# Linear attention block with a squared-ReLU MLP on one core: column parts split on chip, one more tile turned by moves, three tiles normalised on ScalarE

## The chip, the cores and the metric

The kernel runs on one core of a Trainium2 chip. The metric is the time of one execution on the device in microseconds (us): 410.08 us is the median of three runs (409.76 to 411.25). The core has five engines with instruction streams of their own: TensorE (PE in the profile; its weight loads are PEld), VectorE (DVE), ScalarE (ACT), GpSimd (POOL) and SyncE (SP), which here issues nearly all transfers. Each engine works its stream in order; waits between engines are by semaphores.

## What is computed

x is 2048 x 512. It is normalised by rows, goes through a linear attention with 32 heads of 16 channels and, beside it, through an MLP with 1376 hidden units, and the sum of x and both is returned.

```python
xn = layernorm(x)                       # no gain, no bias
q, k, v = xn @ wqkv                     # split in three, 32 heads of 16
phi = lambda t: where(t > 0, t + 1, exp(t)) + 1e-6
kv = einsum("bhsd,bhse->bhde", phi(k), v);  z = phi(k).sum(tokens)
attention = (phi(q) @ kv) / (phi(q) @ z + 1e-6) @ wo
mlp = relu(xn @ w1 + b1)**2 @ w2 + b2
return x + attention + mlp
```

## The kernel before

Float32 products are made from two parts of each factor, a high part (rounded to the TensorE's fp32r form) and a low part (the rest): three matmuls high x high, high x low, low x high. So every operand is "split": a copy on ScalarE makes the high part (`copy("act", ...)`, L111), a subtraction on VectorE or GpSimd the low part (L119, L122).

The 2048 tokens are 16 tiles of 128, in four blocks of four tiles. There are two phases.

Phase 1 (the loop `for i in range(2, NT)`, L801, with tiles 0 and 1 ahead of it) makes, for each tile i:
- statistics (`measure`, L234 and L235, on VectorE), the reciprocal root (`roots`, L245 and L246, mostly on GpSimd), the normalised tile `xp[i]` (`normalise`). In `normalise` tiles below NPE = 8 are normalised on VectorE (L268), the others on ScalarE (L258), for which a short VectorE operation first makes the bias (L254).
- the turned tile (channels on the partitions), needed as "column parts" for the projections. Tiles below NDVE = 4 are turned by TensorE: four transposes (`turned_pe`, L308) into PSUM. The others are turned "by moves": `regroup` (L281) stores the tile to DRAM (`via`), four DMAs (`move`, L289) bring it back with its 32-row blocks in another order into `xg`, and a VectorE transposition of 32x32 blocks (`turn`, L293) finishes it. `transposed` then gives three closures: `high` (ScalarE, L324), `low` (VectorE, L327), and `keep_t`, which stores the turned tile in DRAM (`xTd`, L336) for blocks 0 and 1.
- the projection to k, twelve matmuls (`project`, L369), and phi of it (`phi`: Relu on ScalarE L360, Exp on ScalarE L362, sum on VectorE L364), split in `parts` (L377).
- the token parts (`tokens`: high on ScalarE L111, low on GpSimd L119). The last channel of each normalised tile is first set to one (`ones`, L346, GpSimd), so that the sum of phi(k) comes out of the same product.
- `kx(i)`, twelve matmuls (L389) that add tokens x phi(k) to four PSUM banks.

In round i of the loop TensorE does the projection of tile i and then kx(i - 1); a round is 24 matmuls. The tiles of x come in four loads of two tiles (x8, x10, x12, x14) behind a load of four (x4) and single ones. SyncE issues these loads, the stores and the moves from one queue in program order.

The column parts of a block of four tiles lie in `xsb[0]` or `xsb[1]` (names xs0 and xs1, h and l), which hold two blocks at a time. When a block is done that phase 2 handles second (blocks 0 and 1), its column parts are stored to DRAM (`xsd`, L811, in rounds 4 and 7; 1 MB for each of the four).

Phase 2 (the loop `for n in range(2)`, L941) handles the blocks in pairs, 3 and 2 first, then 1 and 0. For each pair the projection to q and w1 runs as a product of 2x2 blocks with seven instead of eight products (`product`, L488, with operands `aop`, `T`, sums `S`), then squares and splits the hidden chunks (`hidden_2`, L450, L119), multiplies by w2 (`mlp_2`, L130), adds the attention (`add_attention`, L130), the residual (L1054), and stores (L1058). At the end of n = 0 the loop at L1285 walks the hidden chunks of the second block, with steps of other work on ScalarE and VectorE put between by a list (AE). There the operands for n = 1 are prepared: the turned blocks come back from DRAM into `f1` and `f2` (L1254, L1255), from which sums and differences are made (`sums_of`, L671, L111, L122); the column parts are loaded into `x1` and `x2` from `xsd` (L1302); the last chunk of w1 is loaded (L184) and split (`zs`), the first chunk of q is loaded (L714) and split (`operands_first`). The last four steps (L1318) add the attention tile by tile and split the last two hidden chunks (`wait_for`), and the closing loop multiplies those by w2, tile by tile. n = 1 then begins with `plain_1` (pz, L130), which reads x1 and the last chunk of w1, and with the first product (L488).

Of the kernel before, what the change touches and what calls it, by code (L numbers as in the profile page):

```python
# [13 lines left out]
P = 128  # L14
# [4 lines left out]
def kernel(  # L19
# [41 lines left out]
    NPE = 2 * TB  # L61
    NDVE = NPE - 4
    WARM = 11
# [36 lines left out]
    def f32(ap):  # L100
        return ap.bitcast(F32)
# [44 lines left out]
    xTd = [dram.tile([P, NJ, BT], F32, name=f"xTd{b}") for b in range(NB // 2)]  # L146
    xsd = [[dram.tile([P, NJ, BT], F32, name=f"xsd{b}{u}") for u in "hl"] for b in range(NB // 2)]
    w2s, wos = {}, {}
# [99 lines left out]
    def normalise(tiles, st, mv, y):  # L248

        n = len(tiles)  # L250
        r, u = (y[:, k, :n] for k in range(2))
        if tiles[-1] >= NPE:

            nc.vector.scalar_tensor_tensor(u, mv[:, :n, 0], -1.0, r, op0=OP.mult, op1=OP.mult)  # L254
# [7 lines left out]
        for k, i in enumerate(tiles):  # L262
            o, src = xp[i], xr[i]
            if i >= NDVE:

                o, src = o.rearrange("p g (j c) -> p g j c", j=NJ), gjc(src)
            if i < NPE:
                nc.vector.tensor_scalar(o, src, mv[:, k, 0:1], r[:, k:k + 1], op0=OP.subtract, op1=OP.mult)  # L268
                if i in groups:
                    regroup(i)  # L270
            else:
                later.append(lambda a=(i, o, src, k): last(*a))
# [74 lines left out]

    def tokens(i, el="pool"):
        tok[i] = pair(f"tok{i}")
        h, l = tok[i][:, 0], tok[i][:, 1]  # L350
        src = xp[i]
        if i >= NDVE:
            h, l, src = gjc(h), gjc(l), src.rearrange("p g (j c) -> p g j c", j=NJ)
        split(h, l, src, "act", el)
        if NDVE <= i + 1 < NT:
            ones(i + 1)

    def phi(ps, p, mid=lambda: None, late=lambda: None):
# [187 lines left out]
    for i0 in range(0, NT, TB):  # L546
        a = first_xp[i0]
        for k in range(TB):
            xp[i0 + k] = a[:, k]
        if i0 + TB <= NDVE:  # L550
            continue
        n = TB if i0 >= NPE else TB // 2
        if i0 < NPE:
            single = work.tile([P, 2, 512], F32, name=f"xg{i0}s", tag="r0")
            for k in range(2):
                i = i0 + k
                xp[i], xg[i] = (t.rearrange("p (g n) -> p g n", g=NJ) for t in (xp[i], single[:, k]))
                groups[i] = [xp[i], xg[i]]
# [62 lines left out]
    heads_k(3)  # L621
    low1(1)
    for u in range(2):
        some(0, u, (2,))
# [10 lines left out]
    rests_k("dve", 3)  # L635
    fourth = statistics(3)
    roots(*fourth)
    high, low, keep2 = transposed(2)
# [3 lines left out]
    rest(3)  # L642
    load_x(8, x8[:, :2])
    load_x(10, x8[:, 2:])
    load_x(12, two("x12"))
    project(2, pks[2], wk, HL)
    single = group(4)
    soon = group(5)
    normalise(*fourth)
    phi_k(0, pks[0])  # L650
# [5 lines left out]
    normalise(*single)  # L656
    load_x(14, two("x14"))
    parts(1)
    tokens(1, "dve")
    measure(soon)  # L660
    roots(*soon)
    keep2()
# [121 lines left out]

    def small_chunk(z):
        t = raw_1(NF - 1)
        return lambda: split(z[:, 0], z[:, 1], t, "act", "dve")

# [12 lines left out]
    for i in range(2, NT):  # L801
# [4 lines left out]
        move()  # L806
        if i in (4, 7):

            b = i // 7
            for u in range(2):  # L810
                nc.sync.dma_start(xsd[b][u], f32(cols(b * TB)[u]))  # L811
        if i == 9:
# [6 lines left out]
        high = low = keep_t = lambda: None  # L819
        if i < NDVE:  # L820
            high, low, keep_t = transposed(i + 1)
        later = normalise(*soon) if i == 3 else []

        soon_turned = transposed(i + 2) if 11 <= i and i + 2 < NT else ()

        def mid():
            high()
            more(i)

        def late():  # L830
            low()
            more(i)
# [19 lines left out]
        if i != 3:  # L852
            later = normalise(*soon) if soon else []
        parts(i)
        keep_t()
        if i == 2:
            tokens(2)
        if i + 1 < NT:
            tokens(i + 1)
        run(*later)  # L860
        if NDVE < i + 2 < 13:
            run(*transposed(i + 2))
# [3 lines left out]
        if i + 2 in (4, 6, 8, 10):  # L866
            ahead[i + 2] = group(i + 6, i + 7)
        if i < 10:
            measure(ahead[(i + 2) // 2 * 2], i % 2)
        soon = ahead.get(i + 1, ())  # L870
# [70 lines left out]
    for n in range(2):  # L941
# [343 lines left out]
        for e, f in enumerate(waiting[:-2]):  # L1285
# [12 lines left out]
            if e in ((5, 6) if n else (7, 8)):  # L1298
                do(bias)
            if n == 0 and 1 <= e < 5:  # L1300
                k, u = divmod(e - 1, 2)
                nc.sync.dma_start(f32((x1, x2)[k][u]), xsd[(t1, t2)[k] - 2][u])  # L1302
            do(prepare, (1, 0, 0, 1, 0, 2, 2, 3, 1, 3, 1)[e])
            if n == 0:
                if e == 4:
                    z = pair("w1z1")
                    zs = small_chunk(z)
                if e == 5:
                    w = load_1("q", 0)
                if e == 7:  # L1310
                    zs()
            step(AE[e])
# [5 lines left out]
        for k in range(TB):  # L1318
            add_attention(acc, t2 * TB + k, n == 1 and k == last)
            if k < 2:  # L1320
                wait_for(last_two[1 - k])
            if n == 0:
                if k == 0:
                    prepare = operands_first(1, w)
                if k in (0, 2):
                    do(prepare, 2 if k == 0 else 3)
# [43 lines left out]
```

## Time and profile before

| | us |
|---|---|
| median of three runs | 410.08 (409.76 to 411.25) |
| the profiled execution | 410.41 |
| its span | 408.7 |
| TensorE busy | 403.8 |
| VectorE busy | 304.7 |
| ScalarE busy | 262.2 |
| GpSimd busy | 48.5 |
| moved by DMA | 56.87 MB |
| granted TensorE clock (mean) | 0.999 |

The profile is of one execution. Its times are from the start of its span, which is a little shorter than the execution's own time. A line of the timeline has the start, the duration, the engine, the source line, the operation, what is written <- what is read, shapes and a count; in brackets stands how long the engine was idle before and what ended that. SPq is SyncE's issue of a transfer, not the transfer. A line of the chain of waits has start, duration and what was at work.

### The profile page before, as it was taken

To read this page: it belongs to the slowest core of one execution; us is meant where nothing else is said; L and a number is where in the kernel's file an instruction comes from. 1 tells how busy PE (TensorE), PEld (TensorE's weight loads), DVE (VectorE), ACT (ScalarE), POOL (GpSimd) and SP (SyncE) were. 2 spreads that over 40 slices of the span, in tenths; PEclk is the share of its full clock that TensorE was granted. 3 is DMA by queue.
4 is the path that set the end of the run, shared out by engine and by line. 5 is a ranking of instruction groups with operands and counts; after the bars stand their busy time and mean duration, and the time that the engine had idled before them with its cause. 6 is when DMAs were issued, how large, how long until landed. Compare 5 with 4: busy or idle time off the path is not lost.

```text
span 408.7 us, 5630 instructions
## 1 busy us (share of the span) xinstructions
PE 403.8 (99%) x1943; PEld 331.7 (81%) x1943; DVE 304.7 (75%) x556; ACT 262.2 (64%) x459; POOL 48.5 (12%) x81
## 2 busy tenths in 40 slices
PE   8999999999999999999999999999999999999996
PEld 7878888888788888888878887888888888878885
DVE  6886667487898989988349956567989586449833
ACT  4656777556888788886818641677587857837520
POOL 6343333220000000030000300000000200001200
PEclk9999999999999999999999999999999999999999
DMA  6969576810432231381557983321121881024612
GB/s 213 332 210 329 204 309 206 254 31 0 119 91 79 77 103 28 109 204 22 215 204 271 326 194 106 113 53 51 51 79 36 229 189 36 2 103 154 105 26 103
DMA packets 47182, 56.87 MB, mean 139 GB/s; under 512 B 8305, under 2 KB 30577, under 8 KB 45874
## 3 DMA queue, kind: packets, MB, share of 16 engines
q1 hardware_dynamic: 44850, 52.32, 39.3%
q0 software_dynamic: 2304, 4.20, 6.3%
q8 instruction: 15, 0.25, 0.2%
q14 instruction: 13, 0.11, 0.1%
HBM read 41.69 MB, written 13.63 MB: 135 GB/s over the span
## 4 chain that ended last, share of the span: by engine, by line
PE 85%; DMA 6%; DVE 5%; issue 1%; SPq 1%; ACT 1%; POOL 1%; DVEq 0%; ACTq 0%
PE b L488 33%; PE acc L130 29%; PE pk L369 9%; PE kx L389 9%; DMA r<-in_B_w_dram 4%; PE acc L499 2%; PE pz L130 1%; DVE s L119 1%; SPq L289 1%; PE b L130 1%; PE pz0b L130 1%; DMA x<-in_A_x_dram 1%; DMA via<-xp 1%; DMA xg4s<-via 1%; PE pt L308 0%
## 5 line engine op out<-in xcount | busy, mean ns | idle before, releaser
L130 PE MATMUL acc<-w2r,s 128*128 128x512 f32 x477 | 113.1, 390 | 0.4 <-DVE s L119 0.4
L130 PEld LDWEIGHTS acc<-w2r,s 128*128 128x128 f32 x477 | 89.4, 188 | 20.1 <-DVE s L119 0.8
L488 PE MATMUL b<-T,aop 128*128 128x512 f32 x336 | 83.4, 389 | 0.0
L488 PEld LDWEIGHTS b<-T,aop 128*128 128x128 f32 x336 | 63.0, 188 | 13.9 <-ACT t L111 0.8
L1046 POOL DMA_DIRECT2D res<-in_B_b_dram x16 | 14.4, 1091 | 277.2 <-DVE dt L430 87.4
L389 PE MATMUL kx<-pk,tok 128*128 128x512 f32 x192 | 46.3, 390 | 0.0
L389 PEld LDWEIGHTS kx<-pk,tok 128*128 128x128 f32 x192 | 35.9, 188 | 7.6
L488 PE MATMUL b<-xs0h,aop 128*128 128x512 f32 x112 | 36.9, 390 | 0.0
L130 PE MATMUL acc<-mh,aTsr 128*128 128x512 f32 x112 | 35.6, 389 | 0.0
L1054 DVE TENSOR_TENSOR res<-acc,res 128x512 f32<-128x512 f32 x16 | 11.0, 692 | 21.5 <-PE acc L130 19.2
L488 PEld LDWEIGHTS b<-xs0h,aop 128*128 128x128 f32 x112 | 21.0, 188 | 4.4
L130 PEld LDWEIGHTS acc<-mh,aTsr 128*128 128x128 f32 x112 | 21.0, 188 | 4.4
L119 POOL TENSOR_TENSOR tok<-xp,tok 128x512 fp32r<-128x512 f32 x15 | 19.8, 1322 | 38.9 <-ACT tok L111 38.9
L122 DVE TENSOR_TENSOR w2r<-r,w2r 128x512 fp32r<-128x512 f32 (+2 forms) x35 | 23.8, 681 | 0.5 <-ACT w2r L111 0.4
L111 ACT ACTIVATE aop<-S 128x512 fp32r<-128x512 f32 x28 | 17.5, 624 | 9.8 <-DVE S L728 9.8
L119 DVE TENSOR_TENSOR aop<-S,aop 128x512 fp32r<-128x512 f32 x28 | 19.3, 688 | 4.8 <-ACT aop L111 4.4
L119 DVE TENSOR_TENSOR s<-c,s 128x512 fp32r<-128x512 f32 x20 | 13.5, 689 | 11.4 <-ACT s L111 11.3
L488 PE MATMUL b<-xs0l,aop 128*128 128x512 f32 x56 | 21.8, 389 | 0.0
L130 PE MATMUL acc<-ml,aTsr 128*128 128x512 f32 x56 | 21.8, 389 | 0.0
L111 ACT ACTIVATE w2r<-r 128x512 fp32r<-128x512 f32 x32 | 19.6, 620 | 3.0 <-DMA out_dram<-res 2.0
L111 ACT ACTIVATE T<-Tf 128x512 fp32r<-128x512 f32 x16 | 9.5, 624 | 16.1 <-DVE Tf L671 16.0
L488 PE MATMUL b<-xs1h,aop 128*128 128x512 f32 x56 | 19.5, 389 | 0.0
(190 smaller groups left out, 742.9 us busy)
## 6 DMA issues: line engine op xcount, KB each, us to landing
r<-in_B_w_dram SPq DMA_DIRECT2D x49, 256.0 KB, 3.0
res<-in_A_x_dram SPq DMA_DIRECT2D x8, 512.0 KB, 4.2
res<-in_B_b_dram POOLq DMA_DIRECT2D x16, 256.0 KB, 5.8
out_dram<-res SPq DMA_DIRECT2D x15, 256.0 KB, 2.1
via<-xp SPq DMA_DIRECT2D x5, 512.0 KB, 3.2
xg<-via SPq DMA_DIRECT2D x20, 128.0 KB, 2.8
xTd<-t SPq DMA_DIRECT2D x8, 256.0 KB, 3.2
x<-in_A_x_dram SPq DMA_DIRECT2D x4, 512.0 KB, 6.4
```

The source lines that it names most:

```text
L111: nc.scalar.activation(o, i, AF.Copy, bias=bias)
L119: ENG[el].tensor_tensor(out=l, in0=src, in1=f32(h), op=OP.subtract)
L122: nc.vector.tensor_tensor(out=l, in0=src, in1=f32(h), op=OP.subtract)
L130: nc.tensor.matmul(ps, lhsT=a[u], rhs=b[v], start=first and n == 0, stop=last and n == 2)
L289: nc.sync.dma_start(*moves.pop(0))
L369: nc.tensor.matmul(ps, lhsT=cols(i)[u][:, j, slot(i)], rhs=w[v][:, j, :], start=first and n == 0, stop=last and n == len(steps) - 1)
L389: nc.tensor.matmul(kxp[c], lhsT=tok[i][:, u, c * P:(c + 1) * P], rhs=pk[i][:, v], start=i == 0 and (u, v) == first, stop=i == NT - 1 and ( ...
L488: nc.tensor.matmul(ps, lhsT=a[u][:, j * P:(j + 1) * P], rhs=b[v][:, j, :], start=first and j == 0 and n == 0, stop=last and j == 1 and n == 2,
L499: nc.tensor.matmul(ps, lhsT=s[u][:, k * P:(k + 1) * P], rhs=w2s[NF - 1][u][:, a:z], start=first and u == 0, stop=stop and u == 1)
L1046: nc.gpsimd.dma_start(r[:, i], b2[None, :].partition_broadcast(P), accum_op=OP.add)
L1054: nc.vector.tensor_tensor(out=r[:, a:z], in0=ps, in1=r[:, a:z], op=OP.add)
```

## The change

It changes four things.

1. Blocks 0 and 1 keep no column parts in DRAM: the stores at L811 and the loads at L1302 are gone. At the end of n = 0 the column parts are split again from `f1` and `f2`, the turned blocks that are there anyway: `columns_high` (two ScalarE copies of 128x1024 for each block) and `columns_low` (two VectorE subtractions of 128x1024 for each block). The last two hidden chunks are split in other order, both ahead of the operands of n = 1. The last chunk of w1 and the first of q are loaded one step earlier.
2. NDVE becomes 3: tile 3 is turned by moves too. Its statistics, normalisation and moves come ahead of tile 2's column parts.
3. A new bound NACT = 5: tiles 5, 6 and 7 are normalised by ScalarE, tiles 3 and 4 still by VectorE. In round 3 the high part of tile 4 and the normalisations of tiles 6 and 7 follow Exp; in round 2 tile 5 is measured after tile 3's transposition and normalised before `parts`.
4. The loads of x10, x12 and x14 are issued in rounds 2, 3 and 4 behind the moves; x8 behind tile 3's store and in front of its moves. Tiles 8 and 9 are both measured in round 3 (before: 8 in round 2, 9 in round 3).

```diff
-    NDVE = NPE - 4
+    NDVE = NPE - 5
+    NACT = NPE - 3
...
-    xsd = [[dram.tile([P, NJ, BT], F32, name=f"xsd{b}{u}") for u in "hl"] for b in range(NB // 2)]
...
-        if tiles[-1] >= NPE:
+        if tiles[-1] >= NACT:
...
-            if i < NPE:
+            if i < NACT:
                 nc.vector.tensor_scalar(o, src, mv[:, k, 0:1], r[:, k:k + 1], op0=OP.subtract, op1=OP.mult)
...
-    def tokens(i, el="pool"):
+    def tokens(i, el="pool", now=True):
...
-        split(h, l, src, "act", el)
+        copy("act", h, src)
+
+        def low():
+            ENG[el].tensor_tensor(out=l, in0=src, in1=f32(h), op=OP.subtract)
+
+        if now:
+            low()
         if NDVE <= i + 1 < NT:
             ones(i + 1)
+        return low
...
     low1(1)
+    fourth = statistics(3)
+    roots(*fourth)
...
     rests_k("dve", 3)
-    fourth = statistics(3)
-    roots(*fourth)
+    normalise(*fourth)
+    load_x(8, x8[:, :2])
+    move()
     high, low, keep2 = transposed(2)
...
-    load_x(8, x8[:, :2])
-    load_x(10, x8[:, 2:])
-    load_x(12, two("x12"))
...
-    normalise(*fourth)
...
     normalise(*single)
-    load_x(14, two("x14"))
+    token_low = tokens(1, "dve", False)
     parts(1)
-    tokens(1, "dve")
-    measure(soon)
-    roots(*soon)
+    token_low()
     keep2()
...
+    def columns_high(x, t):
+
+        for a in range(0, NJ, 2):
+            copy("act", x[0][:, a:a + 2], t[:, a:a + 2])
+
+    def columns_low(x, t):
+
+        for a in range(0, NJ, 2):
+            rest_of(x[1][:, a:a + 2], t[:, a:a + 2], x[0][:, a:a + 2])
...
-        if i in (4, 7):
-
-            b = i // 7
-            for u in range(2):
-                nc.sync.dma_start(xsd[b][u], f32(cols(b * TB)[u]))
...
-        if i < NDVE:
+        if 2 < i < 5:
+            load_x(2 * i + 6, two(f"x{2 * i + 6}"))
+        if i <= NDVE:
             high, low, keep_t = transposed(i + 1)
+        if i == 2:
+            load_x(10, x8[:, 2:])
+            measure(soon)
+            roots(*soon)
         later = normalise(*soon) if i == 3 else []
...
         def mid():
-            high()
+            if i != 3:
+                high()
             more(i)
 
         def late():
+            if i == 3:
+                high()
+                run(*later)
             low()
...
+        if i == 2:
+            run(*later)
+            later = []
         parts(i)
...
-        run(*later)
-        if NDVE < i + 2 < 13:
+        if i != 3:
+            run(*later)
+        if NDVE < i + 1 < 12:
             run(*transposed(i + 2))
...
-        if i < 10:
-            measure(ahead[(i + 2) // 2 * 2], i % 2)
+        if 2 < i < 10:
+            measure(ahead[(i + 2) // 2 * 2], *((0, 1) if i == 3 else (i % 2,)))
...
-            if n == 0 and 1 <= e < 5:
-                k, u = divmod(e - 1, 2)
-                nc.sync.dma_start(f32((x1, x2)[k][u]), xsd[(t1, t2)[k] - 2][u])
             do(prepare, (1, 0, 0, 1, 0, 2, 2, 3, 1, 3, 1)[e])
             if n == 0:
+                if e == 3:
+                    rawz = raw_1(NF - 1)
                 if e == 4:
                     z = pair("w1z1")
-                    zs = small_chunk(z)
-                if e == 5:
                     w = load_1("q", 0)
+                if e == 6:
+                    columns_high(x2, f2)
                 if e == 7:
-                    zs()
+                    split(z[:, 0], z[:, 1], rawz, "act", "dve")
+                    columns_high(x1, f1)
...
-            if k < 2:
+            if n == 1 and k < 2:
                 wait_for(last_two[1 - k])
             if n == 0:
                 if k == 0:
+                    columns_low(x2, f2)
+                    for f in reversed(last_two):
+                        wait_for(f)
+                    columns_low(x1, f1)
                     prepare = operands_first(1, w)
```

More of the change, by code (lines that the diff above doesn't have):

```diff
@@ L549 @@
             xp[i0 + k] = a[:, k]
-        if i0 + TB <= NDVE:
+        if i0 < TB:
             continue
@@ L553 @@
         if i0 < NPE:
-            single = work.tile([P, 2, 512], F32, name=f"xg{i0}s", tag="r0")
-            for k in range(2):
-                i = i0 + k
+            single = work.tile([P, 3, 512], F32, name=f"xg{i0}s", tag="r0")
+            for k in range(3):
+                i = i0 + k - 1
                 xp[i], xg[i] = (t.rearrange("p (g n) -> p g n", g=NJ) for t in (xp[i], single[:, k]))
@@ L783, in operands_first @@
                 lambda: chunk_split(1, 0, o[1])]
-    def small_chunk(z):
-        t = raw_1(NF - 1)
-        return lambda: split(z[:, 0], z[:, 1], t, "act", "dve")
+    def columns_high(x, t):
[4 more added lines that the diff above has]
+            rest_of(x[1][:, a:a + 2], t[:, a:a + 2], x[0][:, a:a + 2])
     extra, counts = [], [[0, 0, 0, 0, 0, 1, 1, 0, 0, 1, 2, 2, 0, 1, 4, 1, 2]]
```

## The prediction, made before the changed kernel was run

> **What bounds the kernel now.** I read the page's summary first, then the chain of waits for the pitch of the matmuls, then the timeline of TensorE wherever twelve matmuls took longer than that pitch, and last the timelines of the engines that feed those places.
>
> ```profile
> span 408.7 us, 5630 instructions
> ...
> PE 403.8 (99%) x1943; PEld 331.7 (81%) x1943; DVE 304.7 (75%) x556; ACT 262.2 (64%) x459; POOL 48.5 (12%) x81
> ```
>
> TensorE is busy 403.8 of 408.7 us: the rest is the start and the last store. An edit on another engine is worth something only where it moves the start of a matmul. The chain gives the pitch:
>
> ```profile
> 33.63 2.72 PE pk L369 x12
> ```
>
> Twelve matmuls take 2.72 us, 0.2267 each, and from 33.6 us on they follow each other like that nearly everywhere. The exceptions that the change can reach are two. Early, in the timeline (start, duration, engine, line):
>
> ```profile
> 16.27 2.92 PE L389 MATMUL kx<-pk,tok 128*128 128x512 f32 x12
> 19.03 0.60 PE L308 MATMUL pt<-ident,xp 128*128 128x128 f32 x4
> 19.39 3.00 PE L389 MATMUL kx<-pk,tok 128*128 128x512 f32 x12
> ...
> 22.22 0.39 PE L369 MATMUL pk<-wkh,xs1h 128*128 128x512 f32 x1
> ...
> 24.94 2.88 PE L389 MATMUL kx<-pk,tok 128*128 128x512 f32 x12
> 27.89 0.50 PE L369 MATMUL pk<-wkh,xs0h 128*128 128x512 f32 x1
> ...
> 30.75 2.88 PE L389 MATMUL kx<-pk,tok 128*128 128x512 f32 x12
> 33.47 0.39 PE L369 MATMUL pk<-wkh,xs0h 128*128 128x512 f32 x1
> ```
>
> L389 is kx(0), kx(1), kx(2), kx(3); L369 is the projection of tiles 3, 4 and 5; L308 is tile 3's four transposes. From 16.27 to 33.47 lie six groups of twelve, 16.32 us of the 17.20. The other 0.88 is 0.40 for the transposes (19.39 less 16.27 + 2.72) and 0.11, 0.23 and 0.14 in front of or just behind the starts at 22.22, 27.89 and 27.89. Late, at the end of the first half:
>
> ```profile
> 247.18 0.62 PE L130 MATMUL acc<-w2r,s 128*128 128x512 f32 x2
> 248.21 0.50 PE L130 MATMUL acc<-w2r,s 128*128 128x512 f32 x1 [0.41 <-DVE s L119]
> ...
> 252.44 0.39 PE L130 MATMUL pz<-xs0h,w1z 128*128 128x512 f32 x1
> ...
> 247.47 0.69 DVE L119 TENSOR_TENSOR s<-r2c,s 128x512 fp32r<-128x512 f32 x1
> ```
>
> Twenty matmuls lie between 247.18 and 252.44; at the pitch they end at 251.71. TensorE loses 0.73 us there, because the low part of hidden chunk 0 (L119, 247.47) stands on VectorE behind the work for the second half. So all that the change can win is 0.88 + 0.73 = 1.6 us; what it can lose has no such limit.
>
> **The transposes (minus 0.40).** Four matmuls of L308 go; ScalarE's copy of tile 3 out of PSUM for the store goes with them.
>
> **Tile 3's way through the moves.** Its statistics are drawn ahead of tile 2's normalisation, its own normalisation ahead of tile 2's column parts.
>
> ```profile
> 12.46 1.18 PE L369 MATMUL pk<-wkl,xs1h 128*128 128x512 f32 x4
> ...
> 10.68 0.55 DVE L268 TENSOR_SCALAR xp<-x,mv,y 128x512 f32<-128x512 f32 x1 [0.45 <-POOL y L246]
> 11.14 1.29 DVE L574 TENSOR_TENSOR wkl<-rk,wkh 128x512 fp32r<-128x512 f32 x2
> 12.35 0.69 DVE L234 BATCH_NORM_STATS2 st<-x 128x6 f32<-128x512 f32 x1
> 13.07 0.18 DVE L235 BATCH_NORM_AGGREGATE mv<-st 128x2 f32<-128x6 f32 x1
> ...
> 19.28 0.68 DVE L119 TENSOR_TENSOR tok<-xp,tok 128x512 fp32r<-128x512 f32 x1
> ...
> 26.46 0.71 DVE L293 STREAM_TRANSPOSE t<-xg4s 128x512 f32<-128x512 f32 x1 [0.15 <-DMA xg4s<-via]
> ```
>
> VectorE sat idle 0.45 before 10.68; the statistics take 0.69 + 0.18, so what follows shifts by about 0.4: rests 2 and 3 end at 12.9, and tile 3 is normalised at 13.45. TensorE read rest 3 with the third of the four matmuls at 12.46, at 12.9: on the edge, 0 to 0.4, and I take 0. The chain has the two transfers of tile 4:
>
> ```profile
> 18.49 2.36 DMA via<-xp
> ...
> 24.15 2.19 DMA xg4s<-via
> ```
>
> ```profile
> 20.92 3.66 SPq L289 DMA_DIRECT2D xg4s<-via  x4
> ...
> 27.00 1.73 SPq L289 DMA_DIRECT2D xg4s<-via  x4
> ```
>
> The store lands 13.45 + 2.36 = 15.8, the four moves are issued in 1.73 (the second set's rate) and the last lands 2.19 later, 19.75. The transposition on VectorE stands behind token part 1 (19.28 + 0.68) and starts at 19.9. From transposition to first matmul tile 4 needed 27.89 - 26.46 = 1.43: ready at 21.3. TensorE, without transposes, is through kx(1) at 16.27 + 24 x 0.2267 = 21.7. So tile 3 is covered by kx(0) and kx(1) with 0.4 to spare, and its projection starts at 21.7 instead of 22.22. The other end of this cost is the first set's pace: tile 4 took 26.46 - 18.49 = 8.0 from store to transposition, because one of its moves was held in the issue (3.66 for four). At that pace tile 3 is ready 13.45 + 8.0 = 21.4, 1.5 later. I take the fast pace, because in the changed order only one token load of 512 KB is issued ahead of these moves, where three and then a fourth were. On SyncE's queue the five transfers are through at 17.6, before tile 4's store wants it at 18.5, so that store loses nothing; ScalarE's token part of tile 1, now ahead of pk1, fills a wait and moves no matmul.
>
> **ScalarE normalises tiles 5 to 7.** This is what I expect to cost.
>
> ```profile
> 25.14 0.60 ACT L360 ACTIVATE k<-pk 128x512 f32<-128x512 f32 x1 [0.99 <-PE pk L369]
> 27.21 0.63 ACT L324 ACTIVATE xs0h<-t 128x512 fp32r<-128x512 f32 x1 [1.47 <-DVE t L293]
> ...
> 35.47 1.50 ACT L258 ACTIVATE xp<-x,y 128x512 f32<-128x512 f32 x2
> ...
> 26.39 0.70 POOL L246 TENSOR_TENSOR y<-y,power 128x2 f32<-128x2 f32 x1
> ```
>
> Tile 5's statistics now stand behind the transposition: 19.9 + 0.71 + 0.69 + 0.18 = 21.5; its root on GpSimd about 0.8, 22.3; a short VectorE operation and ScalarE's normalisation (0.80 each, 1.50 for two) end at 23.5. On ScalarE behind it wait the high part of pk2 (0.63) and the token part of tile 2 (0.6): 24.7. kx(2) needs both, so it starts at 24.8, where TensorE is free at 24.4. Compared with 24.94 that is still 0.15 early.
>
> The next wait is new. A tile turned by moves gets its column of ones (L346) after the token part of the tile before it on GpSimd. So tile 3's token part on ScalarE waits for GpSimd's subtraction of tile 2 (1.30, like tile 0's at 15.30): 24.7 + 1.3 + 0.1 = 26.1. Queued behind it on ScalarE are the token part (0.6), Relu (0.60) and Exp (0.62) of tile 3, and, now put behind the Exp, the high part of tile 4: 26.1 + 0.6 + 0.6 + 0.6 + 0.6 = 28.45. TensorE waits for that one: the projection of tile 4 starts at 28.5 instead of 27.89, 0.6 later. Tile 4's moves don't decide it (VectorE reaches that transposition at about 26.6 and leaves it at 27.3).
>
> Behind this the pair 6 and 7: root behind GpSimd's subtraction of tile 3 (28.0 + 0.70), normalised on ScalarE at about 30.6, pk3's high part 31.2, and kx(3) starts at 28.5 + 2.72 = 31.2: no new loss. In the next round the statistics of tiles 8 and 9 lie together in front of tile 4's k on VectorE (0.87 more), which puts pk4's high part at 36.9 against kx(4) at 36.7: 0.2. After that every round has its old slack. Early sum: 0.6 + 0.2 = 0.8 us later, the transposes' 0.40 already in it. Bounds: if none of these waits binds, all 0.88 is won; if tile 3 comes 1.5 later, all behind it moves with it, 2.3 lost.
>
> **Token loads behind the moves, and no stores of the column parts.** Tiles 10 to 15 are measured from the fourth round on, a round being 5.44 us; loaded in the first rounds behind the moves of tiles 4 to 7, they are there in time. Zero, and four 1 MB stores less in the moves' way.
>
> **Column parts split on chip.** Four ScalarE copies and four VectorE subtractions of 128x1024 come in, four 1 MB loads go out.
>
> ```profile
> 229.78 1.90 ACT L111 ACTIVATE w2r<-r 128x512 fp32r<-128x512 f32 x3
> 236.25 1.36 ACT L111 ACTIVATE T<-Tf 128x512 fp32r<-128x512 f32 x2 [4.57 <-DVE Tf L671]
> 241.48 0.63 ACT L111 ACTIVATE w1z<-r 128x512 fp32r<-128x512 f32 x1 [3.87 <-DMA r<-in_B_w_dram]
> ...
> 247.45 0.40 ACT L111 ACTIVATE aop<-rq 128x256 fp32r<-128x256 f32 x1
> ...
> 248.67 0.42 DVE L119 TENSOR_TENSOR aop<-rq,aop 128x256 fp32r<-128x256 f32 x1
> ```
>
> No row has the width 1024. From 256 and 512 elements (0.40 and 0.63, 0.42 and 0.69) the slope gives estimates of 1.1 for a copy and 1.2 for a subtraction: 4.4 us on ScalarE, 4.9 on VectorE. Uncovered they would cost TensorE up to that. The cover: ScalarE idles 4.57 before 236.25 and 3.87 before 241.48, VectorE 4.47 before 242.14. That last wait is for the last chunk of w1, and it goes:
>
> ```profile
> 223.29 10.97 SPq L184 DMA_DIRECT2D r<-in_B_w_dram  x3
> ...
> xs1l<-xsd0l SPq DMA_DIRECT2D x1, 1024.0 KB, 14.6
> ```
>
> The chunk's three loads were issued over 10.97 us behind the column loads, the last of which landed 14.6 us after its issue. Without these, at the chunk's usual few us, ScalarE's copy of it can run right behind 237.6 instead of at 241.48, and VectorE's work behind it starts up to 3.9 earlier, with 4.9 of new subtractions in it. VectorE then has: first pair of low parts to about 243, both hidden chunks' low parts by 244.3 (was 248.2), second pair by 246.8, the four chunk sums by 249, and the operand that was split at 248.67 by about 250, the last one by 250.4. TensorE needs hidden chunk 0 at 247.6: the wait goes, minus 0.73. It needs the low column parts from 251.7 and the first operand twelve matmuls later, from 254.4: both there, with 4 to 5 us of slack. Bounds: minus 0.73 or 0; a loss would need the operands over 4 us later.
>
> **Sum.** Plus 0.8 early, minus 0.73 late: plus 0.1. The profiled execution had 410.41 (span 408.7 and 1.7 around it), which becomes 410.5; it lay 0.33 above the median of the runs, 410.08, on which the same sum gives 410.2. About 0.5% (2 us) is what a measurement of this kernel can tell from no change.
>
> **The rivals.**
> 1. The early waits don't bind (GpSimd's column of ones and tile 5's normalisation come a little sooner than I add up): up to 0.88 won, with the late 0.73 up to 1.6: 408.5 to 409.3, say 408.9. For it: each of my waits is only 0.2 to 0.6 long. Against: five in-order steps on ScalarE add up, and none can be left out.
> 2. Slower: tile 3's moves are held by the one token load that is issued in front of them at about 13.9.
>
> ```profile
> x<-in_A_x_dram SPq DMA_DIRECT2D x4, 512.0 KB, 6.4
> ```
>
> At its median it lands at 20.3; moves stuck behind it and landing some 1.5 later (the half of the held set's excess) reach VectorE at 21.8 to 22.5. It decides from 20.3 on, where the 0.4 of slack is gone; 2.0 later on tile 3 moves every round behind it by 2.0 to 2.6, and two tight rounds add a few tenths: plus 2.9 early, minus 0.73 late: 412.3. For it: the held issue in the row at 20.92. Against: the 6.4 is a median under four loads in a row.
> 3. The last chunk of w1 is late all the same (the loads of the next weights keep its queue full): the line from 241.48 stays, the low part of chunk 0 still comes at 248.2, and the late gain is nil: 410.08 + 0.8 = 410.9. Slack of the operands is then still 1 to 3 us, so no loss.
> 4. GpSimd's subtractions slow VectorE down.
>
> ```profile
> 16.16 0.98 DVE L377 SCALAR_TENSOR_TENSOR pk<-k,pk 128x512 fp32r<-128x512 f32 x1
> ...
> 15.30 1.30 POOL L119 TENSOR_TENSOR tok<-xp,tok 128x512 fp32r<-128x512 f32 x1 [1.03 <-ACT tok L111]
> ```
>
> The first pk subtraction ran beside GpSimd's of tile 0 and took 0.98, where the others of that size and kind have about 0.69 (0.68 at 19.28). If the same 0.29 falls on two operations of the new chain, 0.5 or a little more: 410.7. The Trainium skill, "GPSIMD Engine Reference", section "Specifications", says that GpSimd shares its SBUF interfaces with VectorE and contends with instructions that have two SBUF inputs; it speaks against a change that lays more of VectorE's early work beside GpSimd's, and by the row at 16.16 the trace agrees.
>
> **How the numbers follow.** Forecast, 409.6 to 410.9 about 410.2: 0.58. Rival 1: 0.14, of which 0.04 past 408.0 (only with some gain that I don't see). Rival 2: 0.14, nearly all of it past 412.1, with 0.02 more for losses not listed. Rival 3: 0.06. Rival 4: 0.06. Faster by over 0.5% 0.04, slower 0.15, within 0.81. The range takes rival 1's middle and rival 2's time: 408.8 to 412.4.
>
> **What would show it.** In the changed profile: no L308 at 19 us and the projection of tile 3 at 21.7; the transposition of tile 3 starting at about 19.9 with no idle time put down to a transfer; ScalarE idle before tile 3's token part, ended by GpSimd's L346; the projection of tile 4 near 28.5 and of tile 5 near 33.9; no wait of TensorE at 247 to 249, and ScalarE's copy of the w1 chunk not ended by a transfer. I am wrong if the transposition of tile 3 waits for its moves, or if TensorE waits anywhere from 250 to 260.

## The result and the profile after

The changed kernel took 412.84 us, the median of six runs (412.24 to 413.99), against 410.12 for the kernel before in the same series: a ratio of 1.006, 95% interval 1.0048 to 1.0071. It is slower by some 2.7 us, by 0.66% of the medians, where 410.2 (408.8 to 412.4) was forecast. The profiled execution's span is 411.0 us, 2.3 more than before. In the changed kernel the line numbers are some 7 higher: the projection is L376, kx is L396, phi is L367 to L371, the copies are L112, the subtractions L120 and L123, GpSimd's L357.

TensorE does the same work less the four transposes, and the view of what its groups waited for (total us, times, longest) gives the new loss at once:

```profile
PE 403.3 (98%) x1939; PEld 330.4 (80%) x1939; DVE 308.2 (75%) x560; ACT 267.5 (65%) x465; POOL 49.3 (12%) x81
...
PE pk L376 <- ACT xs0h L324: 2.2, 2, 1.5
...
PE kx L396 <- ACT tok L112: 0.2, 1, 0.2
```

TensorE's timeline of the changed kernel has the places. They stand, in the same order, against 22.22, 24.94, 27.89, 30.75 and 33.47 before, and for the last two against kx(4) at 36.19 and the projection of tile 6 at 38.91, which the next fence has:

```profile
21.77 0.39 PE L376 MATMUL pk<-wkh,xs1h 128*128 128x512 f32 x1
...
24.89 3.02 PE L396 MATMUL kx<-pk,tok 128*128 128x512 f32 x12 [0.23 <-ACT tok L112]
28.63 0.50 PE L376 MATMUL pk<-wkh,xs0h 128*128 128x512 f32 x1 [0.72 <-ACT xs0h L324]
...
31.48 2.90 PE L396 MATMUL kx<-pk,tok 128*128 128x512 f32 x12
34.23 0.39 PE L376 MATMUL pk<-wkh,xs0h 128*128 128x512 f32 x1
...
36.97 3.01 PE L396 MATMUL kx<-pk,tok 128*128 128x512 f32 x12
...
41.50 0.50 PE L376 MATMUL pk<-wkh,xs0h 128*128 128x512 f32 x1 [1.52 <-ACT xs0h L324]
```

Up to kx(4) at 36.97 the loss is 0.78, near what the prediction had added up (0.8). Then, within one group, it becomes 2.59: the projection of tile 6 comes at 41.50 instead of 38.91. All that follows in this phase is 2.76 late (52.60 for the same projection that stood at 49.84).

What was late is tile 6's way through the moves. First the kernel before, the timeline of SyncE's queue, of the transposition and of what reads it:

```profile
28.82 0.38 SPq L281 DMA_DIRECT2D via<-xp  x1
29.24 2.89 SPq L336 DMA_DIRECT2D xTd<-t  x2
...
32.23 2.02 SPq L289 DMA_DIRECT2D xg<-via  x4
...
36.19 2.88 PE L389 MATMUL kx<-pk,tok 128*128 128x512 f32 x12
...
37.23 0.71 DVE L293 STREAM_TRANSPOSE t<-xg 128x512 f32<-128x512 f32 x1 [1.46 <-DMA xg<-via]
...
37.98 0.63 ACT L324 ACTIVATE xs0h<-t 128x512 fp32r<-128x512 f32 x1 [1.01 <-DVE t L293]
...
38.91 0.39 PE L369 MATMUL pk<-wkh,xs0h 128*128 128x512 f32 x1
```

Then the changed one:

```profile
23.02 0.43 SPq L159 DMA_DIRECT2D x<-in_A_x_dram  x1
...
23.82 0.34 SPq L281 DMA_DIRECT2D via<-xp  x1
...
28.26 0.70 POOL L246 TENSOR_TENSOR y<-y,power 128x2 f32<-128x2 f32 x1
28.57 1.74 SPq L289 DMA_DIRECT2D xg4s<-via  x4
...
29.20 1.52 ACT L258 ACTIVATE xp<-x,y 128x512 f32<-128x512 f32 x2 [0.62 <-DVE y L254]
...
30.35 0.43 SPq L159 DMA_DIRECT2D x<-in_A_x_dram  x1
...
30.88 0.41 SPq L281 DMA_DIRECT2D via<-xp  x1
...
35.88 1.75 SPq L289 DMA_DIRECT2D xg<-via  x4
...
40.07 0.71 DVE L293 STREAM_TRANSPOSE t<-xg 128x512 f32<-128x512 f32 x1 [2.43 <-DMA xg<-via]
...
40.82 0.63 ACT L324 ACTIVATE xs0h<-t 128x512 fp32r<-128x512 f32 x1 [1.97 <-DVE t L293]
```

The row at 30.35 is the load of x12 (512 KB). It is issued right in front of the store of tiles 6 and 7 at 30.88. The view of the transfers (KB each, us from issue to landing), for the stretch from 28 us, has for the kernel before

```profile
via<-xp SPq DMA_DIRECT2D x1, 512.0 KB, 2.8
```

and for the changed one

```profile
x<-in_A_x_dram SPq DMA_DIRECT2D x1, 512.0 KB, 4.2
via<-xp SPq DMA_DIRECT2D x1, 512.0 KB, 4.9
```

So two things add up in the 2.84 by which the transposition is later (40.07 less 37.23): the store is issued 2.06 later (30.88 less 28.82), and it takes 2.1 longer to land. Two things make the store late, and they end within 0.1 us of each other. ScalarE, behind GpSimd's root, has normalised tiles 6 and 7 at 30.72 (29.20 + 1.52). SyncE's queue is free at 30.78: tile 5's moves were issued at 28.57 instead of 27.00, since tile 5's store at 23.82 stands behind x10's load (23.02) and took 4.7 us to land instead of 2.3, and behind these moves comes x12's load. Something comes back: the moves follow the store's landing at once, where before SyncE was still issuing the two stores of xTd, and they are through sooner.

Late, at the end of the first half, everything went as forecast:

```profile
233.62 2.00 ACT L112 ACTIVATE xs1h<-xT 128x1024 fp32r<-128x1024 f32 x2
...
240.31 0.61 ACT L112 ACTIVATE w1z<-r 128x512 fp32r<-128x512 f32 x1
...
243.37 2.35 DVE L123 TENSOR_TENSOR xs1l<-xT,xs1h 128x1024 fp32r<-128x1024 f32 x2
...
249.97 0.85 PE L131 MATMUL acc<-w2r,s 128*128 128x512 f32 x3
...
254.51 0.39 PE L131 MATMUL pz<-xs0h,w1z 128*128 128x512 f32 x1
```

From the first w2 matmul to pz there are now 4.54 us (254.51 less 249.97), where it took 5.26 (252.44 less 247.18): 0.72 won, twenty matmuls without a wait. ScalarE's copy of the w1 chunk (240.31) is not ended by a transfer. The balance of the profiles: plus 2.76 early, minus 0.72 late, and plus 0.2 behind pz make the 2.3 of the span.

### The profile page after: what moved, and what is told of

Same layout as the page of the kernel before. It is cut to its first block, busy times and chain, and to the rows that moved or that the text cites. A ratio compares the mean times of both kernels' runs of the same rounds, so it can differ in the third digit from the quotient of the medians.

```text
span 411.0 us, 5633 instructions
## 1 busy us (share of the span) xinstructions
PE 403.3 (98%) x1939; PEld 330.4 (80%) x1939; DVE 308.2 (75%) x560; ACT 267.5 (65%) x465; POOL 49.3 (12%) x81
## 4 chain that ended last, share of the span: by engine, by line
PE 89%; DMA 2%; ACT 1%; DVE 0%; SPq 0%; POOL 0%; issue 0%; DVEq 0%
PE acc L131 37%; PE b L495 33%; PE kx L396 7%; PE pk L376 7%; PE acc L506 2%; PE pz L131 1%; DMA via<-xp 1%; DMA xg<-via 1%; PE b L131 1%; PE pz0b L131 1%; ACT xp L258 0%; PE acc L513 0%; PE pkv L927 0%; SPq L289 0%; PE pm L944 0%; DVE t L293 0%
## 5 line engine op out<-in xcount | busy, mean ns | idle before, releaser
L396 PE MATMUL kx<-pk,tok 128*128 128x512 f32 x192 | 46.4, 392 | 0.2 <-ACT tok L112 0.2
L396 PEld LDWEIGHTS kx<-pk,tok 128*128 128x128 f32 x192 | 35.7, 188 | 8.7 <-ACT pk L112 0.7
L112 ACT ACTIVATE aop<-S 128x512 fp32r<-128x512 f32 x28 | 17.5, 625 | 12.6 <-DVE S L732 12.6
L357 POOL TENSOR_TENSOR tok<-xp,tok 128x512 fp32r<-128x512 f32 x15 | 19.8, 1322 | 41.7 <-ACT tok L112 38.8
L123 DVE TENSOR_TENSOR w2r<-r,w2r 128x512 fp32r<-128x512 f32 (+2 forms) x35 | 23.8, 681 | 0.5 <-ACT w2r L112 0.4
L120 DVE TENSOR_TENSOR aop<-S,aop 128x512 fp32r<-128x512 f32 x28 | 19.2, 687 | 4.8 <-ACT aop L112 4.4
L120 DVE TENSOR_TENSOR s<-c,s 128x512 fp32r<-128x512 f32 x20 | 13.6, 688 | 11.4 <-ACT s L112 11.3
L112 ACT ACTIVATE w2r<-r 128x512 fp32r<-128x512 f32 x32 | 19.6, 619 | 2.5 <-DMA out_dram<-res 2.0
L112 ACT ACTIVATE T<-Tf 128x512 fp32r<-128x512 f32 x16 | 9.5, 624 | 14.4 <-DVE Tf L675 14.3
```

Of the source, the lines that this page charges most:

```text
L112: nc.scalar.activation(o, i, AF.Copy, bias=bias)
L120: ENG[el].tensor_tensor(out=l, in0=src, in1=f32(h), op=OP.subtract)
L123: nc.vector.tensor_tensor(out=l, in0=src, in1=f32(h), op=OP.subtract)
L357: ENG[el].tensor_tensor(out=l, in0=src, in1=f32(h), op=OP.subtract)
L396: nc.tensor.matmul(kxp[c], lhsT=tok[i][:, u, c * P:(c + 1) * P], rhs=pk[i][:, v], start=i == 0 and (u, v) == first, stop=i == NT - 1 and ( ...
```

## The experiments

Each run is given with its median, and with the ratio to the kernel before on the same chip and its 95% interval; that kernel's medians were 410.62 (the first four), 410.71 (the next four) and 410.63 (the last three). The theory: the load in front of the store makes the store land late, and tile 6 with it. The rivals: the late normalisation on ScalarE is enough by itself; the wait for GpSimd's column of ones is the cause; or the split of the column parts costs something after all.

### e1: the load taken out of the store's way

```diff
-        if 2 < i < 5:
-            load_x(2 * i + 6, two(f"x{2 * i + 6}"))
+        if i == 4:
+            for k in (12, 14):
+                load_x(k, two(f"x{k}"))
```

> The changed kernel, with the load of tiles 12 and 13 issued behind the moves of tiles 6 and 7 (in round 4, with the load of 14 and 15) instead of in front of their store. Theory A (the 512 KB load issued at 30.35 in front of the store makes the store take 4.9 us instead of 3.3, and that is what made TensorE wait for tile 6): the store lands 3.0 to 3.5 us after its issue, the transposition of tile 6 starts at 38.0 to 38.5 instead of 40.07, its projection at 39.7 to 40.0 instead of 41.50; 1.5 us less than the changed kernel, about 411.3. Theory B (the store is late because ScalarE normalises tiles 6 and 7 late; the load is innocent): the store still takes nearly 5 us, only the 0.4 us of the load's issue comes off: 412.4.

411.52 us, ratio 1.0018 (1.0008 to 1.0028). The store landed in 3.2 us. Rows of SyncE and VectorE in this kernel:

```profile
31.18 0.34 SPq L281 DMA_DIRECT2D via<-xp  x1
...
34.42 1.73 SPq L289 DMA_DIRECT2D xg<-via  x4
36.20 0.94 SPq L159 DMA_DIRECT2D x<-in_A_x_dram  x2
38.74 0.71 DVE L293 STREAM_TRANSPOSE t<-xg 128x512 f32<-128x512 f32 x1 [0.71 <-DMA xg<-via]
```

The store is as late as in the changed kernel (31.18; this profile runs 0.4 late from its first matmuls on), but the moves follow 3.2 behind it instead of 5.0, and TensorE has no wait for tile 6. By the ratios this one load, moved by one round, gives back 0.4 of the 0.6%. Here the queue is free at 30.63 and ScalarE's normalisation (29.63 + 1.52) alone holds the store. That lateness is just covered, since TensorE itself is 0.8 late by then.

### e9: the load alone, put into the kernel before

```diff
-    load_x(12, two("x12"))
+    late_x = two("x12")
...
         high = low = keep_t = lambda: None
+        if i == 3:
+            load_x(12, late_x)
```

> The kernel before, with one edit: the load x12 is issued in round 3 between the moves of tile 5 and the store of tiles 6 and 7, where the changed kernel has it. Everything else, the normalisations too, stays as before. Theory A (a 512 KB load in front of the store is a cause by itself): the store lands about 4.5 to 5 us after its issue (2.8 before), the projection of tile 6 starts 1.3 to 2.1 us later than 38.91, time 411.5 to 412.5. Theory B (the load is only harmful because that store is already late in the changed kernel): the store lands slower, but the transposition of tile 6 waits at most some tenths; projection of tile 6 at most 39.3, time 410.3 to 410.9.

411.83 us, ratio 1.0035 (1.0016 to 1.0055). The kernel before, with nothing changed but this load, has the same picture:

```profile
28.57 0.43 SPq L159 DMA_DIRECT2D x<-in_A_x_dram  x1
29.10 0.41 SPq L281 DMA_DIRECT2D via<-xp  x1
...
34.39 1.74 SPq L289 DMA_DIRECT2D xg<-via  x4
...
38.90 0.71 DVE L293 STREAM_TRANSPOSE t<-xg 128x512 f32<-128x512 f32 x1 [2.96 <-DMA xg<-via]
...
40.33 0.50 PE L369 MATMUL pk<-wkh,xs0h 128*128 128x512 f32 x1 [1.14 <-ACT xs0h L324]
```

The store, now 0.28 later than before, has its moves issued 5.3 us behind it (3.4 before), and TensorE waits 1.14 for tile 6, where it did not wait. The load is a cause by itself, of 1.4 us at that projection (40.33 less 38.91). In this profile the late gap is 1.20 instead of 0.41 as well: ScalarE's copy of the last w1 chunk waited 4.66 for its load, where it had waited 3.87, which is the same 0.79. Why that load came later is open, so not all of the 1.2 us of the medians need be tile 6's.

### e3: two loads in front of the store

```diff
-        if 2 < i < 5:
-            load_x(2 * i + 6, two(f"x{2 * i + 6}"))
+        if i == 3:
+            for k in (12, 14):
+                load_x(k, two(f"x{k}"))
```

> The changed kernel with the suspected cost doubled: the loads of tiles 12, 13 and of 14, 15 are both issued in front of the store of tiles 6 and 7. Theory A: the store lands another 1.3 to 1.6 us later (6.2 to 6.5 after its issue), the projection of tile 6 starts at about 43 instead of 41.5, the time is about 414.3. Theory B: only the issue of one more load, 0.4 us: 413.2.

416.45 us, ratio 1.0133 (1.0113 to 1.0153). TensorE, at the projection of tile 6:

```profile
43.21 0.79 PE L376 MATMUL pk<-wkh,xs0h 128*128 128x512 f32 x1 [3.24 <-ACT xs0h L324]
```

The store took 6.4 us to land and the wait doubled, both as expected: 2.8 with no load in front, 4.9 with one, 6.4 with two. The time is some 2 us worse than expected. The next kx comes at 48.49, 5.28 us behind that projection instead of the usual 2.72, because the granted TensorE clock fell: it is 0.50 in this profile from 43 to 49 us, where the changed kernel's is 1.00 throughout. Of the four executions the one with a mean clock of 1.000 took 415.2; the other three, at 0.991 to 0.996, took 416.2 to 417.2. By this profile the slow clock costs 3.0 us (5.28 for that projection and 3.19 for the kx behind it, less two times 2.72), so it is the larger part of what the expectation missed.

### e4: the split of the column parts alone

The edit is the first part of the change by itself, on the kernel before; the rest of the change is left away.

> The kernel before with the first part of the change alone: the column parts are split on chip, their stores and loads are gone, phase 1 is as before. If the late gain of the changed profile (pz starts 2.07 later than before where the attention's end is 2.79 later) belongs to this part: no wait of TensorE at 247 to 249 and minus 0.7 us, 409.4. Rival: the extra 9 us on ScalarE and VectorE are paid for somewhere else in the first half, or the stores of the column parts at 34 to 57 us held the moves back and their removal helps too: 410.1, or below 409.2.

409.54 us, ratio 0.9967 (0.9955 to 0.998): faster than both kernels. TensorE's only wait in this profile is that behind its warm-up:

```profile
PE warm L518 <- PEq L1360: 0.8, 1, 0.8
```

pz starts at 251.52 instead of 252.44, 0.92 earlier, of which 0.18 was already there at the projection of tile 4 (27.71 for 27.89). So the late term of the sum was right, and all of the loss is in the early parts.

### e2, e5 and e6: who normalises, and where the loads stand

e2 lets VectorE normalise tiles 5 to 7 again (`NACT = NPE`). e5 issues each load right behind a store, in front of that store's moves. e6 does both.

```diff
-        if 2 < i < 5:
-            load_x(2 * i + 6, two(f"x{2 * i + 6}"))
...
         if i == 2:
-            load_x(10, x8[:, 2:])
...
+            load_x(10, x8[:, 2:])
+        if i == 3:
+            load_x(12, two("x12"))
...
+        if i == 4:
+            load_x(14, two("x14"))
```

> The changed kernel with tiles 5 to 7 normalised on VectorE again; loads as in the changed kernel. Theory B: pk2's high part and tile 2's token part come 1.0 earlier, so the projection of tile 4 starts at about 28.0 instead of 28.63; the store of tiles 6 and 7 is issued 1.5 to 2 us earlier (at 29 to 29.4 instead of 30.88), tile 6 is ready before TensorE wants it, and the time is 410.0 to 410.4. Theory A: the store is earlier but still takes 4.9 us behind the load, tile 6's transposition starts at 38.2 to 38.6 and TensorE, free at about 39.0, still waits some 0.8: 411.0.

> The changed kernel with each of the three loads (tiles 10-11, 12-13, 14-15) issued right behind the store of a tile, in front of its moves, instead of in front of the store: while the store lands, the queue waits for it anyway. Theory A (a 512 KB load in front of a store makes the store late): the store of tile 5 lands about 2.4 us after its issue (4.7 in the changed kernel), that of tiles 6 and 7 about 3.3 (4.9), and TensorE's wait for tile 6 goes down from 1.5 to 0.7 or less; 411.0 to 411.4, as with the one load moved. Rival (it is the amount of traffic around the store, wherever it is issued): the load right behind it slows it as much, 412.5 or more.

> As e5_loads_behind, and tiles 5 to 7 normalised on VectorE. This asks for theory B's share with the loads out of the way: the projection of tile 4 at 27.6 (28.63 in the changed kernel), kx(3) at about 30.9, no wait for tiles 5 and 6; with the late gain of 0.7 about 409.6. If the normalisation on ScalarE costs nothing by itself: as e5_loads_behind, 411.2.

e2: 414.46 us, ratio 1.0086 (1.0055 to 1.0118), a miss. Tile 4's wait fell to 0.22, as meant, but tile 5's store, issued 0.5 behind the load of x10 (0.8 in the changed kernel), took 5.3 us to land, and now that decided: tile 5's own transposition waited. VectorE and TensorE of e2:

```profile
34.70 0.71 DVE L293 STREAM_TRANSPOSE t<-xg4s 128x512 f32<-128x512 f32 x1 [3.09 <-DMA xg4s<-via]
...
36.13 0.50 PE L376 MATMUL pk<-wkh,xs0h 128*128 128x512 f32 x1 [2.17 <-ACT xs0h L324]
```

The queue waited with it: tiles 6 and 7 were normalised by 29.03 (28.02 + 1.01), but tile 5's moves could only be issued at 29.57, x12's load followed, and the store went out at 31.88. Part of the 414.46 is the clock again: it is 0.50 from 37.5 to 40.5 us in this profile, and the projection's twelve matmuls took 4.39 us. The one execution of four with a mean clock of 1.000 took 412.74.

e5: 414.05 us, ratio 1.0073 (1.0055 to 1.0092), a miss too, and the more instructive one. The stores land in 2.1 and 2.7 us again, but now the load stands in front of the moves. The transfers and VectorE of e5:

```profile
xg<-via SPq DMA_DIRECT2D x4, 128.0 KB, 6.5
...
42.08 0.71 DVE L293 STREAM_TRANSPOSE t<-xg 128x512 f32<-128x512 f32 x1 [3.90 <-DMA xg<-via]
```

The moves took 6.5 us to land, where they take 2.7 in the changed kernel. "Behind the store" was not enough: now the moves, 1.8 us behind the load, pay in the store's place. They don't pay everywhere: tile 3's four moves (64 KB each) in the changed kernel, 1.9 behind x8's load, landed in 2.0.

e6: 410.68 us, ratio 1.0001 (0.9991 to 1.001), expected 409.6, a miss. The same place of the loads, but the store goes out at 29.05 instead of 31.37, and the moves land in 3.3 us; nothing waits for tile 6, and tile 4's wait is 0.24. With the loads in this place the normalisation on ScalarE costs 3.4 us (414.05 less 410.68). In e2, with the load in front of the stores, going back to VectorE gained nothing (412.74 at the full clock, 412.84 in the changed kernel), because the queue held the store there. The two parts of the change can't be priced one by one.

### e7, e8 and e11: the column of ones made early

In all three the column of ones of tile 3 goes ahead of GpSimd's subtraction of tile 2. e7 is e6 with it, e8 is e5 with it, e11 is e1 with it.

```diff
         copy("act", h, src)
+        if i == 2:
+            ones(3)
...
-        if NDVE <= i + 1 < NT:
+        if NDVE < i + 1 < NT:
             ones(i + 1)
```

> As e6_behind_vector, and tile 3's column of ones set in front of GpSimd's subtraction for tile 2 instead of behind it. Theory C (the column of ones holds ScalarE's token part of tile 3, and through GpSimd's queue the root of tiles 6 and 7): that token part starts at about 23.8 instead of 25.3, the root ends 0.9 us earlier, the projection of tile 4 starts at 27.3, that of tile 5 at 32.8 instead of 33.5 in the kernel before; 408.9 to 409.1, the fastest of all. Without C: as e6_behind_vector, 409.6.

> As e5_loads_behind (tiles 5 to 7 on ScalarE), and the column of ones early. Theory C: the token part of tile 3 starts right behind that of tile 2 (24.8 instead of 26.3); the projection of tile 4 is then held by its transposition on VectorE and starts at 28.3 instead of 28.63; the root of tiles 6 and 7 comes 0.7 earlier, their store at about 30.1, and the wait for tile 6 nearly goes: 409.8 to 410.3. Without C: as e5_loads_behind, 411.2.

> The changed kernel with both small repairs: x12 and x14 behind the moves of tiles 6 and 7, and tile 3's column of ones made on GpSimd before its subtraction of tile 2. The wait of 0.72 for tile 4 should shrink to 0.3 or less, the transposition of tile 6 not wait for a transfer: 410.6 to 411.1. If it stays at 411.5 the column of ones was worth nothing here.

e7: 410.15 us, ratio 0.9983 (0.9974 to 0.9992). e8: 412.0 us, 1.0032 (1.0019 to 1.0045). e11: 411.14 us, 1.0015 (1.0005 to 1.0024). e7 and e8 are misses, by 1 us and by 2; e11 is at the edge of its range, but the wait for tile 4 did not shrink. In none of them does ScalarE wait for L346 any more, and yet the projection of tile 4 still waits: 0.42 in e7, 0.87 in e8, 0.90 in e11. Now tile 4's transposition on VectorE is late, and the reason is a row in front of it. In e8:

```profile
24.99 2.54 POOL L359 TENSOR_TENSOR tok<-xp,tok 128x512 fp32r<-128x512 f32 x2 [2.12 <-ACT tok L112]
...
26.77 0.83 DVE L245 TENSOR_SCALAR y<-mv 128x2 f32<-128x2 f32 x1
27.48 0.70 DVE L293 STREAM_TRANSPOSE t<-xg4s 128x512 f32<-128x512 f32 x1
```

and in the changed kernel:

```profile
26.69 0.17 DVE L245 TENSOR_SCALAR y<-mv 128x2 f32<-128x2 f32 x1
...
26.90 0.71 DVE L293 STREAM_TRANSPOSE t<-xg4s 128x512 f32<-128x512 f32 x1
```

With the early column of ones GpSimd's two subtractions run back to back, and the small VectorE operation of 128x2 (L245), which took 0.17 where GpSimd stood idle, takes 0.83: it ends with GpSimd's work (26.77 + 0.83 = 27.60; 24.99 + 2.54 = 27.53). In e7 and e11 it takes 0.83 too, and in the kernel before, where the two subtractions also ran back to back (23.71 + 2.54 = 26.25), it took 0.63 (25.68 + 0.63 = 26.31). So the early ones free ScalarE and hold VectorE 0.66 longer. What remains of the gain: 0.5 us where VectorE normalises (e6 to e7, 410.68 to 410.15); 2 us from e5 to e8, where the store goes out 1.1 sooner (30.28 for 31.37, though 0.5 of it is a later start of e5's profile), its moves land in 4.9 instead of 6.5, and tile 6's wait falls from 2.98 to 0.76; between e1 and e11 nothing, their intervals overlap.

### e10: the load on another queue

```diff
-        if 2 < i < 5:
-            load_x(2 * i + 6, two(f"x{2 * i + 6}"))
+        if i == 4:
+            load_x(14, two("x14"))
...
-                run(*later)
+                later[0]()
+                load_x(12, two("x12"), nc.scalar)
+                run(*later[1:])
```

> The changed kernel; the load x12 is issued by ScalarE, between the normalisations of tiles 6 and 7, at about 30.0 us, so ahead of the store by as much as before but on another queue. If the order in SyncE's queue holds the store, it lands in 2.8 to 3.3 us, the projection of tile 6 starts at about 40.2, time 411.3 to 411.6. If the transfers share the engines whatever their queue, it lands in 4.5 to 5 us still, the projection of tile 6 starts at 41.3 to 41.9, time 412.6 to 413.2 (ScalarE's own issue of the load adds some tenths).

413.25 us, ratio 1.0068 (1.0044 to 1.0091). ScalarE issued the load at 29.64, SyncE the store at 31.18. In the view of the transfers:

```profile
x<-in_A_x_dram ACTq DMA_DIRECT2D x1, 512.0 KB, 4.0
via<-xp SPq DMA_DIRECT2D x1, 512.0 KB, 3.8
```

3.8 lies between the two forecasts, the time is that of the second, and the load was 1.5 us ahead of the store instead of 0.5, so part of it may have passed. The transposition of tile 6 waited 2.13 for its moves and TensorE 1.17, and a wait of 0.40 at kx(4) is new. The run doesn't tell whether the queue or the engines behind it hold the store; the load in this place on another queue gained nothing.

## Why the prediction was wrong

**The step that failed.** It is "Token loads behind the moves": "loaded in the first rounds behind the moves of tiles 4 to 7, they are there in time. Zero". I asked only when the loaded tiles are wanted, and they were there in time. I did not ask what is issued right behind each load. Behind x12 stands the store of tiles 6 and 7. This load costs that store 1.7 us of landing by e1 (4.9 less 3.2) and 2.5 by e9 (5.3 less 2.8), and TensorE 1.5 and 1.1 of wait at tile 6; e3 shows that a second load costs more. Behind x10 stands the store of tile 5, whose late moves hold the queue; e2 shows that this alone makes the next store late.

**The second half of it** is "After that every round has its old slack". The prediction had tiles 6 and 7 normalised "at about 30.6" (30.7 in the profile), and used it for kx(3) only. Followed on to the store, it gives 30.88, 2.06 later than the 28.82 of the kernel before. The row at 37.23 of the profile before, which the prediction does not use, showed that tile 6 was tight there: its transposition had waited 1.46 for a transfer, and TensorE read its result, from the copy's end near 38.6, about 0.3 later. The two halves together make the 1.8 by which the early loss was mis-sized (2.59 at tile 6, less 0.78).

**Rival 2 had the mechanism and the wrong load.** It priced moves "held by the one token load that is issued in front of them" at 412.3, for x8 and tile 3. There it did not come: tile 3's transposition started at 19.92 without a wait for a transfer (forecast 19.9). The load landed in 3.5 us, and the moves 1.9 behind it in 2.0. Behind x10 and x12 stood stores, half a microsecond to 0.8 behind, and these were held; in the same text I set those two loads at zero. Its time was close to the result by luck, for a loss that it had put 20 us too early.

**What held, with the profile after.** The transposes: gone, projection of tile 3 at 21.77 (21.7 forecast), so the fast pace was the right end. ScalarE's order: kx(2) at 24.89 (24.8), and tile 3's token part held by GpSimd as reckoned (26.28, forecast 26.1):

```profile
26.15 0.09 POOL L346 MEMSET xp<- 128x1 f32 x1
...
26.28 0.63 ACT L112 ACTIVATE tok<-xp 128x512 fp32r<-128x512 f32 x1 [1.44 <-POOL xp L346]
```

Then the projection of tile 4 at 28.63 (28.5), kx(3) at 31.48 (31.2), the projection of tile 5 at 34.23 (33.9), kx(4) 0.78 late (0.8). That this last sum agrees so well is partly luck: tile 4's wait alone gave 0.74 of it (28.63 less 27.89) instead of 0.6, and the 0.2 reckoned at kx(4) did not come, since TensorE got there at the same moment as pk4's high part (36.28 + 0.63 = 36.91). The column split: 0.72 won (0.73), copies of 1.0 (1.1) and subtractions of 1.2 (1.2), no wait from 250 to 260; e4 shows the gain by itself.

**The other rivals.** Rival 1 (the early waits don't bind): refuted by the waits of 0.23 and 0.72. Rival 3 (the last chunk of w1 late anyway): refuted at 240.31. Rival 4: VectorE's pk subtraction beside GpSimd's took 0.99 again, but at the same place as before, at 16.20, and in the changed kernel no VectorE operation of the new chain was stretched. It cost nothing there; that it is real shows in e7, e8 and e11.

**What stays open.** Whether queue or engines hold the store (e10); why the clock fell after TensorE's waits of 3.24 in e3 and 2.17 in e2, and not after 2.98 in e5's profile; why the last w1 chunk landed later in e9's.

## What to carry to other kernels

A load costs nothing only if it has nothing tight behind it: for each transfer that is moved, name the next two or three in the queue and the slack of whoever reads them, not only when its own data is wanted. A wait "ended by a transfer" in the profile before, even one that costs TensorE nothing, marks the place where the slack is least, so price the change there first. And when a mechanism is taken up as a rival for one place, price it at every place where the change makes the same pattern.

## What the runs showed of the hardware

- The 512 KB store of tiles 6 and 7 landed in 2.7 to 3.3 us from its issue with no load close in front (before, e1, e4 to e8, e11), in 4.9 to 5.5 with one 512 KB load issued half a microsecond before it (after, e2, e9), in 6.4 with two (e3). The 256 KB store of tile 5 took 2.1 to 2.3 with none close in front (before, e5 to e8) and 4.0 to 5.3 with such a load issued 0.5 to 0.8 before it (after, e1 to e3, e10, e11). The loads in front of these stores landed in 4.0 to 5.6.
- A VectorE operation on 128x2 elements took 0.83 us while GpSimd subtracted, and 0.17 while it was idle (after, e1 to e3, e5, e6, e10); it ended when GpSimd's subtraction did (e7, e8, e11). The statistics of 128x512 beside the same subtraction kept 0.66 to 0.69. The Trainium skill, "GPSIMD Engine Reference", section "Specifications", names, beside instructions with two SBUF inputs, those in a 2-port performance mode as contending; a one-input operation that is held agrees with that as far as it goes, but no run here shows the mode.
- Tile 6's four moves of 128 KB landed in 2.6 to 3.3 us with no load close in front, and with a 512 KB load issued 1.8 us in front of them in 6.5 (e5) and 4.9 (e8).
- After a wait of TensorE of 3.24 us (e3) the granted clock was 0.50 for about 6.8 us, after 2.17 (e2) for about 3.4; after 2.98 in e5's profile it stayed at 1.00. At 0.50 twelve matmuls took 5.28 us instead of 2.72 (e3).
- ScalarE's copy of 128x1024 took 1.04 us and VectorE's subtraction 1.22 (after), each 0.2 less than two of the half size (0.63 and 0.69 each).
